# Splitting the first quarter of w1 into a free buffer ahead of the experts, loading the second tile's rows later, and re-dealing the routing turns

## The chip, the cores and the metric

One core of one Trainium2 chip runs the whole program. The metric is the device time of one execution in microseconds (us). A core has five engines with queues of their own: TensorE (PE, with its weight loads PEld), VectorE (DVE), ScalarE (ACT), GpSimd (POOL) and SyncE (SP), which here issues the plain DMAs. POOL issues the indirect ones. Each queue runs in order.

## The reference

Attention with a bias, then a mixture of experts with one expert for each token. q, k, v are (8, 8, 576, 64); the 4608 tokens have 512 columns; there are 8 experts with w1 (512 x 1024) and w2 (1024 x 512).

```python
scores = scale * q @ k.T + bias            # bias from positions: log1p, a 32-wide hidden layer, 8 heads
attn = softmax(scores); x = attn @ v       # rows of 512 columns, one for each token
logits = x @ w_gate + modality_bias[modality_id]
e_idx = argmax(logits); gate = softmax(logits)[e_idx]
for e in range(8):                         # only the rows with e_idx == e
    out[mask] = gate[mask] * (relu(x[mask] @ w1[e]) @ w2[e])
```

## The kernel before, in words

**Attention.** The kernel works on 32 pairs of heads, four pairs for each of the 8 batches. The loop of `attention` takes a pair in five turns (u = 0 to 4) and runs one turn past the last pair: pair 32 only finishes the products with v of pair 31. What PE, ACT, DVE, POOL and SP do in a turn is written out by hand in `ORDER`; letters X and B in it give a turn to the routing of the batch before. Extra work of the last pairs is hung on turns by `first_tiles`, which fills a table (pair, u) -> functions.

**Routing.** For each batch `route_steps` gives two lists: PE steps (X: two logits steps, two transposes of the logits, the rank, five `s_rows`) and other steps (B: reciprocal, top, one-hot, gate, position, and for the last batch the tables of the experts' tiles). A step waits for a given number of steps of the other list. `s_rows(c)` transposes 128 rows of x (64 for c = 4), scales them on POOL and scatters them by an indirect DMA (L904) into `xg`, a table in HBM sorted by expert. All accesses to `xg` at rows known only at run time are ordered one after the other: a scatter waits until the transfer before it has landed, a load of rows (L1125) waits for the scatters before it, and a later scatter waits for that load.

**Experts.** Tiles of 256 rows: K = 5 first tiles, which hold only rows of the first seven batches, run in `moe_first`, with the routing of the eighth batch dealt out among them. Then `moe_rest` runs the others. `load_rows(t)` (SP, L1125) brings 256 rows of `xg`; `xprep` transposes them on PE (L1202) and splits them into a high and a low part, `xh` on ACT (L1205) and `xl` on DVE (L1206). These lie in the two buffers QT[0] and QT[1], which attention used for q; tile t takes number t % 2. The weights are split the same way into `whi` and `wlo`. `phase1` makes the hidden layer in four pieces (f2 = 0 to 3) of 24 matmuls (L1221), each followed by a relu on ACT (L1223) and its low part on DVE (L1224). `phase2` (L1238) makes two halves of 128 rows with 24 matmuls each; between them stands `xprep` of the next tile. After phase 1 the next tile's w1 is split (four casts on ACT and four subtractions on DVE, L1185 and L1186).

**The first tile's w1** has no phase before it in which to be split. So `wsplit_cols(part)` splits one quarter of its columns at a time (256 of 1024, which is what one f2 needs): the cast on ACT at L1192, the subtraction on DVE at L1193. `tile(0)` calls it for parts 0 and 1 ahead of f2 = 0, for part 2 ahead of f2 = 1 and for part 3 ahead of f2 = 2. The target `whi`, `wlo` lies in the pool "mp", which takes the memory of attention's own pool (Eb, eT, the rows `xrb` that are scattered from, and others). The first use of the new pool waits for every user of the old one, the last scatter's DMA among them.

**The routing turns of the first tiles** are the list `steps` in `moe_first`: six entries for a tile, one behind each f2, one behind the first half of phase 2 and `xprep`, one behind the second half. B and X give a turn to the lists above, F writes one of nine fills (`fill_steps`): one blank block, and behind each expert's last row one tile of blank rows (L1151 on SP).

**Sums over experts.** `s_cum` in `table` and `s_keep` form running sums over 8 values with one copy and seven one-element additions on DVE (L1014, L1016, L1081, L1083).

Of the kernel before, what the change touches and what calls it, by code (L numbers as in the profile page):

```python
# [11 lines left out]
F32 = mybir.dt.float32  # L12
# [9 lines left out]
P = 128  # L22
# [7 lines left out]
E = 8  # L30
# [80 lines left out]
class Attn:  # L111
# [819 lines left out]
    def moe_early(self, cp):  # L931

        nc = self.nc
        lo, hi = n_tiles(self.n_tok)
        self.n_kt = self.n_tab // TS - 1
        self.T = hi
        self.sure = lo
        n_tt = max(E, hi + 1 - self.K)
        one = cp.tile([1, 2 * E + self.n_kt + n_tt], F32, name="one")
        nc.sync.dma_start(one, self.io["c_one"])  # L940
        self.eb, self.iota = one[:, 0:E], one[:, E : 2 * E]
        self.kt, self.tt = one[:, 2 * E : 2 * E + self.n_kt], one[:, 2 * E + self.n_kt :]
        self.gates = cp.tile([P, 4], F32, name="gates")
        self.gk = cp.tile([1, E, self.n_kt], F32, name="gk")
        self.ge = cp.tile([1, n_tt, E], F32, name="ge")
        self.tf = cp.tile([1, 4, n_tt], F32, name="tabf")
        self.ev = {nm: cp.tile([1, E], F32, name=nm) for nm in ("cnt", "off", "nt", "cum", "val", "taken", "start", "big")}
        self.ex = cp.tile([1, 1], F32, name="last_expert")
        nc.vector.memset(self.ex, -1.0)
        nc.vector.memset(self.ev["taken"], 0.0)  # L950
        self.tabs = {nm: cp.tile([1, 4, n], I32, name=f"tab_{nm}") for nm, n in (("first", max(1, self.K)), ("big", hi + 1 - self.K), ("tiny", E))}
        self.idt = cp.tile([P, 4], I32, name="idt")
        self.tab_end = cp.tile([1, E], I32, name="tab_end")
        self.ids_q = [cp.tile([P, 1], I32, name=f"idsq{k}") for k in range(NT)]
        self.quad = cp.tile([P, 1], F32, name="quad")
        nc.sync.dma_start(self.quad, self.io["c_quad"])

        slots = self.NBm.rearrange("p (c q h) k -> p c q (h k)", c=4, q=NP)
        w = [slots[:, :, q, 0 : 2 * DM] for q in range(NP)]
        rest = [slots[:, :, q, 2 * DM : 2 * S] for q in range(NP)]  # L960
        self.wst, self.ws = [w[0], w[1]], [w[2], w[3]]
        self.xr = [slots[:, c, 2, XW * j : XW * j + XW] for c, j in ((0, 0), (1, 0), (3, 0), (0, 1), (1, 1))]
        self.lt = slots[:, 2, 2, 0:XW]
        self.hq = [rest[0], rest[3]]
        self.gx = [self.NBr[:, k : k + 2, 0:XW] for k in (0, 2)]
        d = self.n_pair % 2
        qt = [self.QT[k].rearrange("p a w -> p (a w)") for k in (d, 1 - d)]
        self.xh = [t[:, 0 : NDC * TS].rearrange("p (c w) -> p c w", c=NDC) for t in qt]
        self.xl = [t[:, NDC * TS : 2 * NDC * TS].rearrange("p (c w) -> p c w", c=NDC) for t in qt]
# [19 lines left out]
    def counts(self, out, least):  # L989
# [9 lines left out]
        )  # L999
        V.tensor_reduce(out, self.gk, axis=AX.X, op=ALU.add)  # L1000

    def table(self, nm, nt, start):


        V, ev = self.nc.vector, self.ev
        tab = self.tabs[nm]
        T = tab.shape[2]
        TE = [1, T, E]
        f, ge, tt = self.tf[:, :, 0:T], self.ge[:, 0:T, :], self.tt[:, 0:T]
        row = lambda t: t.rearrange("p (o e) -> p o e", o=1).to_broadcast(TE)  # L1010
        col = lambda t: t.rearrange("p (t o) -> p t o", o=1).to_broadcast(TE)

        def s_cum():
            V.tensor_copy(ev["cum"], nt)  # L1014
            for e in range(1, E):
                V.tensor_tensor(ev["cum"][:, e : e + 1], ev["cum"][:, e : e + 1], ev["cum"][:, e - 1 : e], op=ALU.add)  # L1016
            V.tensor_tensor(ev["val"], nt, ev["cum"], op=ALU.subtract)
            V.scalar_tensor_tensor(ev["val"], ev["val"], float(TS), start, op0=ALU.mult, op1=ALU.add)
            V.tensor_tensor(ev["val"], ev["val"], self.eb, op=ALU.add)

        def s_expert():
            V.tensor_tensor(ge, col(tt), row(ev["cum"]), op=ALU.is_ge)
            V.tensor_reduce(f[:, 0, :], ge, axis=AX.X, op=ALU.add)
            V.tensor_scalar(f[:, 3, :], f[:, 0, :], E - 0.5, None, op0=ALU.is_lt)
            V.tensor_scalar(f[:, 0, :], f[:, 0, :], E - 1.0, None, op0=ALU.min)

        def s_row():
            V.tensor_tensor(ge, col(f[:, 0, :]), row(self.iota), op=ALU.is_equal)
            V.tensor_tensor(ge, ge, row(ev["val"]), op=ALU.mult)
            V.tensor_reduce(f[:, 1, :], ge, axis=AX.X, op=ALU.add)  # L1030
            V.scalar_tensor_tensor(f[:, 1, :], tt, float(TS), f[:, 1, :], op0=ALU.mult, op1=ALU.add)
            if nm != "tiny":
                V.tensor_tensor(f[:, 1, :], f[:, 1, :], f[:, 3, :], op=ALU.mult)
                return

            empty = float(E * self.n_tab)
            V.scalar_tensor_tensor(f[:, 1, :], f[:, 1, :], -empty, f[:, 3, :], op0=ALU.add, op1=ALU.mult)
            V.tensor_scalar(f[:, 1, :], f[:, 1, :], empty, None, op0=ALU.add)
            V.tensor_copy(tab[:, 0:2, :], f[:, 0:2, :])
            V.tensor_copy(tab[:, 3, :], f[:, 3, :])  # L1040

        def s_new():
            V.tensor_tensor(f[:, 2, 0:1], f[:, 0, 0:1], self.ex, op=ALU.is_equal)
            if T > 1:
                V.tensor_tensor(f[:, 2, 1:T], f[:, 0, 1:T], f[:, 0, 0 : T - 1], op=ALU.is_equal)
            V.tensor_scalar(f[:, 2, :], f[:, 2, :], -1.0, 1.0, op0=ALU.mult, op1=ALU.add)
            V.tensor_tensor(f[:, 2, :], f[:, 2, :], f[:, 3, :], op=ALU.mult)
            V.tensor_copy(self.ex, f[:, 0, T - 1 : T])
            V.tensor_copy(tab, f)

        return [s_cum, s_expert, s_row] + ([s_new] if nm != "tiny" else [])
# [17 lines left out]
    def last_tables(self):  # L1069
# [8 lines left out]
            V.tensor_tensor(ev["nt"], ev["cnt"], ev["start"], op=ALU.is_gt)  # L1078

        def s_keep():  # L1080
            V.tensor_copy(ev["cum"], ev["nt"])  # L1081
            for e in range(1, E):
                V.tensor_tensor(ev["cum"][:, e : e + 1], ev["cum"][:, e : e + 1], ev["cum"][:, e - 1 : e], op=ALU.add)  # L1083
            V.tensor_tensor(ev["big"], ev["big"], ev["nt"], op=ALU.add)
            V.scalar_tensor_tensor(ev["nt"], ev["cum"], NT + 0.5, ev["nt"], op0=ALU.is_lt, op1=ALU.mult)
            V.tensor_tensor(ev["big"], ev["big"], ev["nt"], op=ALU.subtract)
# [101 lines left out]
    def wsplit_cols(self, part):  # L1188

        sl = slice(TS * part, TS * part + TS)  # L1190
        w, h, l = self.wst[0][:, :, sl], self.whi[0][:, :, sl], self.wlo[0][:, :, sl]
        self.nc.scalar.copy(h, w)  # L1192
        self.nc.vector.tensor_tensor(l, w, h.bitcast(F32), op=ALU.subtract)  # L1193

# [13 lines left out]
    def phase1(self, t, before, beside):  # L1208
        nc = self.nc
        xh, xl = self.xh[t % 2], self.xl[t % 2]  # L1210
        hh, hl = self.hh, self.hl
        hi, lo = self.whi[0], self.wlo[0]
        for f2 in range(NFC // 2):
            before(f2)
            ps = self.ring("p1")
            for a in range(2):
                f = 2 * f2 + a
                fs = slice(P * f, P * f + P)
                ops = [(w, x, c) for w, x in ((hi, xh), (hi, xl), (lo, xh)) for c in range(NDC)]
                for i, (w, x, c) in enumerate(ops):  # L1220
                    nc.tensor.matmul(ps[:, a, :], w[:, c, fs], x[:, c, :], start=i == 0, stop=i == len(ops) - 1)  # L1221
            sl = slice(2 * f2, 2 * f2 + 2)
            nc.scalar.activation(hh[:, sl, :], ps, AF.Relu)  # L1223
            nc.vector.scalar_tensor_tensor(  # L1224
                hl[:, sl, :], ps, 0.0, hh[:, sl, :].bitcast(F32), op0=ALU.max, op1=ALU.subtract
            )
            beside()
# [28 lines left out]
    def tile(self, t, beside=None, between=()):  # L1256
# [10 lines left out]
        def ahead(f2):  # L1267
            for f in itertools.islice(between, 1):
                f()
            if t:  # L1270
                return
            for part in {0: (0, 1), 1: (2,), 2: (3,)}.get(f2, ()):
                self.wsplit_cols(part)
            if f2 == 2:
                self.load_new(1, 0)
# [20 lines left out]
    def first_tiles(self):  # L1296
# [12 lines left out]
        add(3, 0, lambda: self.load_w("first", 0, 1, self.wst[1]))  # L1309
        for w in range(2):  # L1310
            add(4, w, lambda w=w: self.xprep(0, w))
        if self.K > 1:
            add(4, 0, lambda: self.load_rows(1))
        return at

    def route_rest(self):
# [5 lines left out]
    def moe_first(self):  # L1322


        steps = iter("B,X,X,X,X,B,B,X,B,B,X,X,X,X,X,B,BF,BFF,BF,BF,BF,BF,BBF,BF".split(","))

        def beside():
            for op in next(steps, ""):
# [2 lines left out]
                    f()  # L1331

        self.fills = iter(self.fill_steps())
        if self.K:
            self.moe_load(1)
        for t in range(self.K):
# [166 lines left out]
```

## Time and profile before

| | |
|---|---|
| time, median of 3 runs | 1111.91 us (1110.93 to 1113.19) |
| the profiled execution's own time | 1110.05 us |
| its span, first to last instruction | 1108.1 us |
| mean granted TensorE clock | 0.990 of full speed |
| DVE, ACT, POOL busy | 764.6, 647.9 and 316.5 us |

All rows below are of this one execution; their times are us from the start of its span. Attention ends and the experts begin around 640 us. The first five tiles start phase 1 at 645.5, 674.4, 704.4, 729.1 and 752.5 us. In a timeline a row has its start, its length, the engine, the line, the operation, output <- input, the shape, the count, and in brackets the engine's idle time before it with what ended it. A letter q behind an engine's name is its queue.

### The profile page before, as it was taken

What the parts mean: (1) busy time and instruction counts of PE and PEld (TensorE: products, weight loads), DVE (VectorE), ACT (ScalarE), POOL (GpSimd) and SP (SyncE); (2) the same over time, 40 slices, a digit from 0 to 9 for tenths busy, and PEclk for the clock granted to TensorE, in tenths of its full rate; (3) what the DMA queues carried; (4) which work ended last, traced back from release to release, by engine and by line L of the source; (5) the groups of instructions that cost most, each with busy time, mean ns of one, the idle gap of its engine ahead of it and who ended that gap; (6) DMA issues with size and microseconds to landing.
All of it is one profiled execution on the core that took longest, in us unless ns stands there. A gap on an engine that the chain in (4) does not pass through costs nothing.

```text
span 1108.1 us, 23130 instructions
## 1 busy us (share of the span) xinstructions
PE 1062.6 (96%) x8324; PEld 890.5 (80%) x8324; DVE 764.6 (69%) x1682; ACT 647.9 (58%) x1250; POOL 316.5 (29%) x546
## 2 busy tenths in 40 slices
PE   7989999999999999999999978999999999999994
PEld 3457888878788887878777868899999999889894
DVE  7976678787687877867778655697555654454553
ACT  7766766666675766666666643454555544454542
POOL 0003425525345344363452411421101011111010
PEclk9999999999999999999999989999999999999998
DMA  6994444536445353544444601134113721243310
GB/s 167 223 191 98 122 112 109 149 82 166 95 122 135 100 149 96 131 126 123 119 125 109 215 24 39 68 132 156 55 39 114 273 71 57 75 164 108 122 40 22
DMA packets 88765, 128.09 MB, mean 116 GB/s; under 512 B 30753, under 2 KB 55585, under 8 KB 88643
## 3 DMA queue, kind: packets, MB, share of 16 engines
q1 hardware_dynamic: 82626, 107.58, 36.2%
q0 software_dynamic: 5920, 18.95, 4.8%
q8 instruction: 68, 1.11, 0.4%
q14 instruction: 55, 0.44, 0.1%
q10 hardware_dynamic: 96, 0.00, 0.0%
HBM read 135.62 MB, written 23.44 MB: 144 GB/s over the span
## 4 chain that ended last, share of the span: by engine, by line
PE 81%; DVE 5%; DMA 5%; POOL 5%; issue 2%; ACT 2%; SPq 0%; POOLq 0%; ACTq 0%; DVEq 0%
PE p L1221 18%; PE p L1238 17%; PE xps L545 12%; PE sps L453 10%; PE eps L497 7%; PE xps L402 4%; PE xps L539 3%; PE bps L199 3%; POOL qs L384 2%; DMA xg<-xrb,pos 1%; DMA NBm<-xTb 1%; PE eps L503 1%; PE xps L1202 1%; POOL xg L904 1%; DVE Eb L468 1%
## 5 line engine op out<-in xcount | busy, mean ns | idle before, releaser
L482 ACT ACTIVATE Eb<-Eb,mn 128x576 f32<-128x576 f32 x288 | 222.8, 776 | 146.8 <-DVE mn L468 144.8
L453 PE MATMUL sps<-KT,QT 128*128 128x288 f32 x1152 | 204.2, 312 | 4.5 <-DVE mn L468 2.8
L468 DVE CUSTOM_DVE_ANT_0 Eb<-sps,NBm 128x576 f32<-128x576 f32 x256 | 185.6, 753 | 10.7 <-issue 4.3
L1221 PE MATMUL p<-QT,w1hi 128*128 128x256 f32 x1152 | 165.4, 287 | 6.0 <-ACT w1hi L1192 6.0
L453 PEld LDWEIGHTS sps<-KT,QT 128*128 128x128 f32 x1152 | 161.7, 189 | 10.1 <-issue 3.4
L1221 PEld LDWEIGHTS p<-QT,w1hi 128*128 128x128 f32 x1152 | 151.0, 194 | 10.9 <-ACT w1hi L1192 6.5
L1224 DVE SCALAR_TENSOR_TENSOR hl<-p,hh 128x512 fp32r<-128x512 f32 x72 | 49.7, 691 | 152.9 <-ACT hh L1223 152.7
L497 PE MATMUL eps<-idf,Eb 128*128 128x128 f32 x1024 | 143.8, 275 | 0.0
L545 PE MATMUL xps<-eT,vraw 128*64 128x288 f32 x1024 | 141.8, 412 | 0.5 <-DVE KT L340 0.5
L1247 POOL DMA_INDIRECT out<-mo,idt x36 | 41.6, 1156 | 320.3 <-ACT QT L1205 225.1
L487 POOL COPY rem<-Eb 128x128 f32<-128x128 f32 x128 | 36.9, 295 | 315.9 <-ACT Eb L482 315.5
L497 PEld LDWEIGHTS eps<-idf,Eb 128*128 128x128 f32 x1024 | 113.5, 140 | 6.2 <-DVE mn L468 5.0
L338 ACT ACTIVATE eT<-eps 128x512 f32<-128x512 f32 x160 | 94.2, 590 | 41.0 <-PE eps L497 41.0
L1223 ACT ACTIVATE hh<-p 128x512 fp32r<-128x512 f32 x72 | 43.0, 598 | 125.1 <-PE p L1221 122.4
L1238 PE MATMUL p<-w2hi,hh 128*128 128x512 f32 x288 | 114.0, 396 | 0.0
L1238 PE MATMUL p<-w2hi,hl 128*128 128x512 f32 x288 | 112.5, 390 | 0.0
L545 PEld LDWEIGHTS xps<-eT,vraw 128*64 128x64 f32 x1024 | 65.2, 136 | 48.4 <-issue 12.3
L340 DVE COPY xTb<-xps 128x288 f32<-128x288 f32 x64 | 29.2, 457 | 107.5 <-PE xps L545 61.6
L1186 DVE TENSOR_TENSOR w2lo<-NBm,w2hi 128x1024 fp32r<-128x1024 f32 x72 | 88.2, 1225 | 16.4 <-ACT w2hi L1185 16.4
L1221 PE MATMUL p<-QT,w1lo 128*128 128x256 f32 x576 | 93.6, 285 | 0.0
L340 DVE COPY eT<-eps 128x512 f32<-128x512 f32 x128 | 84.6, 682 | 0.0
L1186 DVE TENSOR_TENSOR w1lo<-NBm,w1hi 128x1024 fp32r<-128x1024 f32 x72 | 83.2, 1218 | 0.0
(227 smaller groups left out, 1842.1 us busy)
## 6 DMA issues: line engine op xcount, KB each, us to landing
NBm<-moe_w SPq DMA_DIRECT2D x23, 2048.0 KB
NBm<-moe_w SPq DMA_DIRECT2D x44, 1024.0 KB
QT<-QT SPq DMA_DIRECT2D x64, 304.0 KB
NBr<-xg SPq DMA_DIRECT2D x20, 516.0 KB
NBm<-xTb SPq DMA_DIRECT2D x32, 288.0 KB
KH<-KT SPq DMA_DIRECT2D x64, 144.0 KB
qraw<-q SPq DMA_DIRECT2D x32, 256.0 KB
kraw<-k SPq DMA_DIRECT2D x32, 256.0 KB
```

Source lines behind the costliest of these rows:

```text
L338: self.nc.scalar.activation(out, ps, AF.Copy, scale=scale)
L340: self.nc.vector.tensor_copy(out, ps)
L402: nc.tensor.transpose(pr[:, j, :], xs[:, 4 * (part % 2) + j, :, :].rearrange("p a d -> p (a d)"), self.idr)
L453: nc.tensor.matmul(ps[:, half, :], q, k[:, HS * half : HS * half + HS], start=i == 0, stop=i == len(terms) - 1, skip_group_check=True,)
L468: nc.vector.tensor_tensor_reduce(out=e.rearrange("p (t w) -> p t w", t=2), in0=ps, in1=nb.rearrange("p (t w) -> p t w", t=2), scale=1.0, s ...
L482: self.nc.scalar.activation(e, e, AF.Exp, bias=mn, scale=-1.0, accum_out=sm)
L497: nc.tensor.transpose(ps[:, k, :], e[:, part, P * k : P * k + P], self.idf)
L545: nc.tensor.matmul(ps[o, :], v[:, h, k, :], self.eT[:, h, k, sl], start=half == 1 and k == 0, stop=half == 0 and k == 3, tile_position=(0, ...
L1186: self.nc.vector.tensor_tensor(l, w, h.bitcast(F32), op=ALU.subtract)
L1221: nc.tensor.matmul(ps[:, a, :], w[:, c, fs], x[:, c, :], start=i == 0, stop=i == len(ops) - 1)
L1224: nc.vector.scalar_tensor_tensor(hl[:, sl, :], ps, 0.0, hh[:, sl, :].bitcast(F32), op0=ALU.max, op1=ALU.subtract)
L1238: nc.tensor.matmul(ps, h[:, f, sl], m[:, f, :], start=i == 0, stop=i == len(ops) - 1)
```

## The change

Four edits, which stand in the diff below.

1. **First quarter of w1.** Part 0 is split no longer into `whi[0]`, `wlo[0]` but into `xh[1]`, `xl[1]`, that is the buffer QT[1], and this is called at turn (32, 3), in front of the last products with v. `phase1` reads this buffer for f2 = 0 of tile 0. Part 1 alone is split ahead of f2 = 0.
2. **Rows of the second tile.** `load_rows(1)` moves from turn (32, 0) to the start of `moe_first`, behind all scatters of the seventh batch.
3. **Routing turns.** The list `steps` of `moe_first` is dealt out anew. By tile, before: (B,X,X,X,X,B) (B,X,B,B,X,X) (X,X,X,B,BF,BFF) (BF,BF,BF,BF,BBF,BF); after: (B,X,X,X,-,X) (BB,-,X,B,B,X) (X,X,X,X,BBF,BBFF) (BF,BF,BF,BF,BBF,BF).
4. **Running sums.** Three additions of 8 values, shifted by 1, 2 and 4 within zero-padded rows, replace the copy and seven additions. Three small memsets are added in `moe_early`.

```diff
+        self.pad = [cp.tile([1, 4 + E], F32, name=f"pad{k}") for k in range(3)]
+        for t in self.pad:
+            nc.vector.memset(t, 0.0)
+        self.ev["nt"] = self.pad[0][:, 4:]
...
+    def running(self):
+        n, a, b = self.pad
+        for out, x, k in ((a[:, 4:], n, 1), (b[:, 4:], a, 2), (self.ev["cum"], b, 4)):
+            self.nc.vector.tensor_tensor(out, x[:, 4:], x[:, 4 - k : 4 - k + E], op=ALU.add)
...
-            V.tensor_copy(ev["cum"], nt)
-            for e in range(1, E):
-                V.tensor_tensor(ev["cum"][:, e : e + 1], ev["cum"][:, e : e + 1], ev["cum"][:, e - 1 : e], op=ALU.add)
+            self.running()
...
-        w, h, l = self.wst[0][:, :, sl], self.whi[0][:, :, sl], self.wlo[0][:, :, sl]
+        w = self.wst[0][:, :, sl]
+        h, l = (self.whi[0][:, :, sl], self.wlo[0][:, :, sl]) if part else (self.xh[1], self.xl[1])
...
+            early = t == 0 and f2 == 0
+            hi, lo = (self.xh[1], self.xl[1]) if early else (self.whi[0], self.wlo[0])
...
-            for part in {0: (0, 1), 1: (2,), 2: (3,)}.get(f2, ()):
+            for part in {0: (1,) if self.K else (0, 1), 1: (2,), 2: (3,)}.get(f2, ()):
...
-        if self.K > 1:
-            add(4, 0, lambda: self.load_rows(1))
+        add(4, 3, lambda: self.wsplit_cols(0))
...
-        steps = iter("B,X,X,X,X,B,B,X,B,B,X,X,X,X,X,B,BF,BFF,BF,BF,BF,BF,BBF,BF".split(","))
+        steps = iter("B,X,X,X,,X,BB,,X,B,B,X,X,X,X,X,BBF,BBFF,BF,BF,BF,BF,BBF,BF".split(","))
...
         self.fills = iter(self.fill_steps())
+        if self.K > 1:
+            self.load_rows(1)
```

## Rows read from the trace of the kernel before

**Rows 1.** The page's busy times: us, share of the span, instructions
```profile
PE 1062.6 (96%) x8324; PEld 890.5 (80%) x8324; DVE 764.6 (69%) x1682; ACT 647.9 (58%) x1250; POOL 316.5 (29%) x546
```

**Rows 2.** Stretches: length, busy PE, PEld, DVE, ACT, POOL, clock, DMA share, GB/s
```profile
639.50:645.50 6.00, 0.02 (x1) 0.00 (x0) 0.46 (x1) 1.07 (x2) 1.26 (x3) 0.71 0.16 45
645.50:647.50 2.00, 1.98 (x9) 1.98 (x10) 2.00 (x2) 0.92 (x1) 0.00 (x0) 0.50 0.00 0
647.50:649.50 2.00, 2.00 (x14) 2.00 (x14) 0.36 (x1) 0.00 (x0) 0.00 (x0) 0.66 0.00 0
...
680.30:682.10 1.80, 0.19 (x2) 0.10 (x1) 1.53 (x10) 1.53 (x2) 0.22 (x1) 1.00 0.00 0
682.10:684.10 2.00, 1.97 (x13) 1.97 (x13) 1.97 (x5) 0.00 (x0) 0.00 (x0) 0.72 0.03 8
684.10:686.10 2.00, 2.00 (x11) 2.00 (x11) 0.12 (x2) 0.00 (x0) 0.00 (x0) 0.50 0.00 0
```

**Rows 3.** Timeline of the passage from attention to the experts
```profile
635.70 0.18 POOL L903 COPY xrb<-gi 64x4 f32<-64x4 f32 x1
...
636.03 0.22 ACT L338 ACTIVATE rT<-eps 128x64 f32<-128x64 f32 x1 [0.66 <-PE eps L508]
...
636.94 0.46 DVE L340 COPY xTb<-xps 128x288 f32<-128x288 f32 x1 [1.83 <-PE xps L545]
...
638.77 0.75 PE L539 MATMUL xps<-rT,vrem 128*128 128x288 f32 x2
...
641.37 0.95 POOL L904 DMA_INDIRECT xg<-xrb,pos  x1 [5.49 <-DMA NBr<-xg]
...
644.43 1.99 ACT L1192 CAST w1hi<-NBm 128x1024 fp32r<-128x1024 f32 x2 [8.17 <-DMA xg<-xrb,pos]
...
645.52 2.08 PE L1221 MATMUL p<-QT,w1hi 128*128 128x256 f32 x8 [6.01 <-ACT w1hi L1192]
```

**Rows 4.** The chain that ended last, in order of time: start, us, what
```profile
622.30 6.33 DMA xg<-xrb,pos
...
636.64 3.94 DMA NBr<-xg
...
652.98 1.00 PE xps L800 x8
...
752.61 11.51 PE p L1221 x96
```

**Rows 5.** Timeline, DVE in the first tile: first hl, and w1's last quarter
```profile
650.77 0.69 DVE L1224 SCALAR_TENSOR_TENSOR hl<-p,hh 128x512 fp32r<-128x512 f32 x1 [2.91 <-ACT hh L1223]
...
656.97 1.22 DVE L1193 TENSOR_TENSOR w1lo<-NBm,w1hi 128x1024 fp32r<-128x1024 f32 x1
```

**Rows 6.** Timeline of PE: transposes of routing that waited in tiles 0 and 1
```profile
668.77 0.33 PE L823 MATMUL xps<-idf,lt 128*128 128x128 f32 x1 [1.55 <-DVE QT L1206]
...
698.05 0.66 PE L893 MATMUL xps<-idf,xTb 128*128 128x128 f32 x4 [2.06 <-DVE QT L1206]
```

**Rows 7.** Timeline: running sums on DVE, and PE behind the first of them
```profile
576.93 2.36 DVE L1016 TENSOR_TENSOR cum<-cum 1x1 f32<-1x1 f32 x7
...
580.64 1.48 PE L453 MATMUL sps<-KT,QT 128*128 128x288 f32 x8 [1.66 <-DVE mn L468]
...
729.61 1.24 DVE L1083 TENSOR_TENSOR cum<-cum 1x1 f32<-1x1 f32 x7
```

**Rows 8.** Timeline of tiles 2 to 4: scatters, fills, the sixth tile's rows
```profile
707.82 1.01 POOL L904 DMA_INDIRECT xg<-NBm,pos  x1 [0.28 <-POOL NBm L903]
...
724.39 1.78 POOL L904 DMA_INDIRECT xg<-NBm,pos  x1 [1.43 <-DMA xg<-NBm,pos]
...
729.58 0.38 SPq L1141 DMA_DIRECT2D xg<-NBm  x1
...
763.26 0.63 SPq L1125 DMA_DIRECT2D NBr<-xg  x1
...
769.43 0.82 PE L1202 MATMUL xps<-idf,NBr 128*128 128x128 f32 x6
```

More of the change, by code (lines that the diff above doesn't have):

```diff
@@ L946, in moe_early @@
         self.tf = cp.tile([1, 4, n_tt], F32, name="tabf")
-        self.ev = {nm: cp.tile([1, E], F32, name=nm) for nm in ("cnt", "off", "nt", "cum", "val", "taken", "start", "big")}
+        self.ev = {nm: cp.tile([1, E], F32, name=nm) for nm in ("cnt", "off", "cum", "val", "taken", "start", "big")}
+        self.pad = [cp.tile([1, 4 + E], F32, name=f"pad{k}") for k in range(3)]
+        for t in self.pad:
+            nc.vector.memset(t, 0.0)
+        self.ev["nt"] = self.pad[0][:, 4:]
         self.ex = cp.tile([1, 1], F32, name="last_expert")
@@ L1080, in s_keep @@
         def s_keep():
-            V.tensor_copy(ev["cum"], ev["nt"])
-            for e in range(1, E):
-                V.tensor_tensor(ev["cum"][:, e : e + 1], ev["cum"][:, e : e + 1], ev["cum"][:, e - 1 : e], op=ALU.add)
+            self.running()
             V.tensor_tensor(ev["big"], ev["big"], ev["nt"], op=ALU.add)
@@ L1211, in phase1 @@
         hh, hl = self.hh, self.hl
-        hi, lo = self.whi[0], self.wlo[0]
         for f2 in range(NFC // 2):
             before(f2)
+            early = t == 0 and f2 == 0
+            hi, lo = (self.xh[1], self.xl[1]) if early else (self.whi[0], self.wlo[0])
             ps = self.ring("p1")
@@ L1217, in phase1 @@
                 f = 2 * f2 + a
-                fs = slice(P * f, P * f + P)
+                fs = slice(P * (f % 2 if early else f), P * (f % 2 if early else f) + P)
                 ops = [(w, x, c) for w, x in ((hi, xh), (hi, xl), (lo, xh)) for c in range(NDC)]
```

## The prediction

> **What bounds the kernel now.** I read the busy times first: TensorE is busy 1062.6 of 1108.1 us [rows 1], so only what makes PE idle or slow can move the time, and the reader should look for the rest of 45 us. [...] The timeline and the chain tell why the passage is idle [rows 3, 4]. The second tile's rows are loaded as soon as the last scatter but one has landed, from 636.64 for 3.94 us, to 640.58; POOL, ready with the last scatter's rows at 635.88, waits 5.49 us for that load and scatters at 641.37; ACT casts at 644.43 what PE needs at 645.52. Meanwhile PE's last product with v ends at 638.77 + 0.75 = 639.52. Two more waits are transposes of routing behind DVE: 1.55 and 2.06 us [rows 6]. In the attention part one wait of 1.66 us follows the running sums [rows 7]. From 704 us on the tiles run without a gap: 96 products of phase 1 in 11.51 us, 2.88 for a piece of 24 [rows 4].
>
> **The change part by part.** The sum goes against the profiled execution, 1110.05 us (span 1108.1 and 1.95 around it); the median shown is 1.86 above that, and I add the sum to the median.
>
> *Passage, edits 1 and 2.* The cast of part 0 writes a buffer outside the old pool. ACT is free from 636.25 [rows 3]; a cast takes 1.0 (half of 1.99), so it is done at 637.3. DVE copies until 637.40, then subtracts for 1.22 [rows 3, 5], to 638.6. Both are hidden by the last products, which end at 639.52; without this cover they would cost 2.2. The next DVE copy of attention waits for PE until after 639.5 anyway. So the first products can follow at once: of the 6.0 idle us 0.1 stay, **-5.9**. PE doesn't pause, so the slow clock behind the gap goes as well: 2.0 x (1 - 0.50) + 2.0 x (1 - 0.66) = 1.7 [rows 2], **-1.7**.
>
> What is late next is part 1, still behind the old pool. Without the load in between, the last scatter starts 0.8 us after the landing that let the load go at 636.6 (as at 641.37 behind 640.58), at 637.4; from its start to the cast took 3.06 us [rows 3], so the cast begins at 640.5 and ends at 641.5, the subtraction at 642.7. PE has finished the first piece at 639.5 + 2.9 = 642.4 and needs the low part 1.0 us later: in time by 0.9 and 0.7. Behind that DVE is the tight engine: from its first hl to the end of the last quarter it worked 658.19 - 650.77 = 7.4 us [rows 5]. Now hl starts 0.6 us behind the first piece, at 643.0, and the last quarter is ready at 650.4; PE, after two pieces (5.8) and both logits steps (1.0 for the first [rows 4]; the second has an eighth of its columns, I take 0.3), needs it at 642.4 + 7.1 + 1.0 = 650.5. Even, so I put **+0.3**; bounds 0 and 2.7 (the last scatter taking 6.33, as one did [rows 4], instead of about 3).
>
> The load itself goes behind the scatter, 640.2 to 644.1; on SP nothing is queued behind it before tile 0's own transfers, and its reader `xprep(1)` comes after all of phase 1. Nothing.
>
> *Routing turns, edit 3.* In tile 0 the transpose that stood behind `xprep` and waited for the subtractions of w1 and xl now stands behind the second half of phase 2, when DVE is long done: **-1.55** [rows 6]. In tile 1 the rank came one piece behind the one-hot and PE waited: 1.80 - 0.19 = 1.6 idle, and 2.0 x 0.28 + 2.0 x 0.50 = 1.56 lost to the clock [rows 2]. Now top and one-hot both stand behind the first piece and the rank two pieces, 5.8 us, after it. DVE must do hl (0.7), one subtraction (1.2) and twelve small operations, which at the ten in 1.53 of [rows 2] and gaps between them are some 2.6 us; with the relu before them that is 5.2. In time by about 0.5; I leave 0.3 for a wait: **-2.9**, bounds -3.2 and -1.6 (a wait as long, without the fall of the clock). In tile 1 the first rows of the last batch leave the place behind `xprep`, where they waited 2.06 for xl: **-2.1** [rows 6].
>
> This has a price. The scatters of the last batch begin one turn later. Of the five, the second now takes the place that the third had, and the last has one more in front of it in tile 2. From the scatter at 707.82 to the last at 724.39 there are three steps in 16.57 us, one load of rows (3.94) among them [rows 4, 8]: 4.2 for a scatter. Behind the last one hangs a chain without slack: POOL's blank block, stored at 729.58, eight fills and two loads of rows on SP, the second at 763.26, landed about 767.2; PE transposes these rows at 769.43 [rows 8]. The slack is 2.2, and tile 2 grows by four transposes (0.66 at most [rows 6], I take 0.4). So PE will wait 4.2 - 2.2 - 0.4 = **+1.6** in tile 4; bounds 0 and 5.
>
> *Running sums, edit 4.* Seven additions take 1.24 us when undisturbed, 0.177 each [rows 7]; a copy and seven become three, five fewer, 0.9 us. Two of the three places are hidden in tiles that PE bounds. The first, at 576.93, is followed by a PE wait of 1.66 on DVE: **-0.9**, bounds 0 and -1.66 (there the seven took 2.36). [...] The three memsets, where PE waits for DVE once, cost **+0.1** (0 to 0.3, by the same 0.177 at most for two of them).
>
> Sum: -5.9 - 1.7 + 0.3 - 1.55 - 2.9 - 2.1 + 1.6 - 0.9 + 0.1 = **-13.05**. The profiled execution goes from 1110.05 to 1097.0, the median from 1111.91 to **1098.9**.
>
> **The rivals.**
> (a) *The chain of scatters and fills is longer than 4.2 more.* Each later link adds to the wait in tile 4, and from about 1 us more also to that for tile 4's own rows. With 3 us more: 1101.9; with 5: 1103.9. For it: there is no slack in the chain; against: single steps of it were even.
> (b) *Part 1 comes late.* The last scatter takes 6.33 us, the cast starts at 643.8 and the second piece 2.4 to 2.7 us late: 1101.5. Against it: the last one itself took 3.06 with all waits behind it [rows 3].
> (c) *The early quarter does not do what it says*, because PE's first product waits for the scatter all the same (its PSUM bank too was attention's). Then the products start at 640.5 rather than 639.6, or, if the early cast itself is held, at 641.5: 1099.8 to 1100.8.
> (d) *Slower.* The scatters of the last batch and the fills behind them get slow as a whole: five scatters at 6.33 in place of about 3.06 are 16 us more, all of it waited for before the sixth tile's transposes: 1115. It decides from 13 us of added delay, 0.8 us for each of the 16 links; between 11 and 15 there is no change to be measured. For it: one scatter did take 6.33 [rows 4]; against: the steps in tile 2 averaged 4.2 with issue and landing [rows 8], and nothing in the change adds traffic beside them. [...]
>
> **How the numbers follow.** The forecast has 0.62, its own range is 1096.5 to 1101. Rival (a) has 0.15, (b) 0.10, (c) 0.06, (d) 0.07. All bounds at their best give -16.3 (1095.6), all but (d) at their worst about -4 (1108). The range 1095.5 to 1104.5 takes in the forecast, most of (a), (b) and (c), and leaves out (d) and the far ends. What a measurement can tell from no change is 0.2%, 2.2 us. Only (d) reaches that: 0.03 for no change, 0.04 for slower, 0.93 for faster.
>
> **What would show it.** Right: the first L1221 starts within 0.3 us of the last L539, at about 639.5, clock 1.00 there; the last scatter near 637.4 with no wait for a load; L823 and the rank without idle time before them; a new wait of PE at the L1202 of tile 4, for the load of rows. Wrong: a PE gap over 1 us between the first two pieces (b); a first product at 640.5 or later (c); any clock below 1.00 between 640 and 700; a wait of more than 4 us in tiles 3 to 4 (a, d). If tile 2's start does not move by 14 us or so, the sum fails before the chain is reached.

## The result, and the profile after

The changed kernel takes 1101.74 us (median of 4 runs, 1101.56 to 1102.27), the kernel before 1112.11 beside it (4 runs, 1110.93 to 1113.19): ratio 0.9908, 95% interval 0.9891 to 0.9925. It is faster by some 10 us; the forecast of 1098.9 was 2.8 us too low, the range held it. The profiled execution took 1102.27 us (span 1100.5), 7.8 less than the one profiled before, where the sum of the prediction, which is worked against that execution, has 13.05 less.

In the busy times little is to be seen: the busy line of the page, to be read against [rows 1], has PE 1.7 us and DVE 2.7 us less.

```profile
PE 1060.9 (96%) x8324; PEld 889.9 (81%) x8324; DVE 761.9 (69%) x1665; ACT 647.6 (59%) x1250; POOL 318.9 (29%) x546
```

The timeline of the passage answers to [rows 3].

```profile
635.20 1.04 ACT L1199 CAST QT<-NBm 128x1024 fp32r<-128x1024 f32 x1
635.57 0.95 POOL L904 DMA_INDIRECT xg<-xrb,pos  x1 [1.37 <-DMA xg<-xrb,pos]
...
637.78 0.75 PE L539 MATMUL xps<-rT,vrem 128*128 128x288 f32 x2
638.15 3.25 PE L1229 MATMUL p<-QT,QT 128*128 128x256 f32 x24
...
638.61 1.05 ACT L1199 CAST w1hi<-NBm 128x1024 fp32r<-128x1024 f32 x1 [2.37 <-PE xps L539]
```

The early cast is done at 636.24, POOL no longer waits for the second tile's rows (5.49 us before), and the first piece of the experts follows the last product with v at once. No gap is left there.

The chain that ended last shows what took its place. It is PE from 638 to 716, and then no longer PE: it goes over POOL (an output scatter of 1.97 us, with the blank rows behind it) and SP into the row table's transfers, and comes back to PE at 760.22. Columns: start, us, what.

```profile
638.53 5.75 PE p L1229 x48
...
672.70 0.04 PE xps L871
...
717.68 1.97 POOL out L1255
...
720.80 0.38 SPq L1147
...
728.61 3.92 DMA NBr<-xg
...
752.29 3.75 DMA xg<-NBm
...
756.17 4.00 DMA NBr<-xg
760.17 0.04 issue
760.22 1.97 PE xps L1209 x8
```

The rank (L871) is a link of 0.04 us in PE's own chain, with no wait. Two PE waits are new, both at the transposes of a tile's rows: in tile 3 for those of tile 4, in tile 4 for those of tile 5 (timeline of PE):

```profile
732.58 1.97 PE L1209 MATMUL xps<-idf,NBr 128*128 128x128 f32 x8 [2.60 <-DMA NBr<-xg]
...
760.22 1.97 PE L1209 MATMUL xps<-idf,NBr 128*128 128x128 f32 x8 [2.62 <-DMA NBr<-xg]
```

The stretches around them, with the columns of [rows 2]:

```profile
642.00:644.00 2.00, 2.00 (x20) 2.00 (x18) 1.69 (x2) 1.92 (x3) 0.00 (x0) 1.00 0.00 0
...
730.60:732.60 2.00, 0.02 (x1) 0.02 (x1) 1.08 (x1) 2.00 (x3) 0.00 (x0) 0.91 0.61 223
732.60:734.20 1.60, 1.60 (x9) 1.60 (x9) 1.60 (x3) 1.60 (x2) 0.00 (x0) 0.50 0.33 110
734.20:736.20 2.00, 2.00 (x8) 1.63 (x7) 2.00 (x3) 1.67 (x4) 0.52 (x1) 0.64 0.46 171
760.20:762.00 1.80, 1.78 (x9) 1.79 (x10) 1.80 (x2) 1.80 (x3) 0.00 (x0) 0.50 0.71 235
762.00:764.00 2.00, 2.00 (x8) 1.64 (x8) 2.00 (x3) 1.32 (x3) 0.88 (x1) 0.76 0.01 5
```

In the passage the granted clock is now 1.00; behind each new wait it is 0.50, then 0.64 behind the first and 0.76 behind the second. Each wait is paid 1.6 times: tiles 3 and 4 take 27.61 and 27.47 us from the first piece of one to that of the next, 4.3 and 4.2 more than before, for waits of 2.6.

By the starts of phase 1 (before: in the section on its profile, and 775.76 for tile 5; after: 638.15, 663.82, 687.71, 712.84, 740.45, 767.92) tile 2 begins 16.7 us earlier, tile 5 only 7.8. From there on both have the same pace, 23.3 us a tile.

Why the chain was late shows in POOL's and DVE's timeline of tile 2:

```profile
699.70 1.46 POOL L904 DMA_INDIRECT xg<-NBm,pos  x1 [4.13 <-DMA NBr<-xg]
...
703.85 5.76 POOL L904 DMA_INDIRECT xg<-NBm,pos  x1 [1.49 <-DMA xg<-NBm,pos]
704.10 4.61 DVE L1192 TENSOR_TENSOR w1lo<-NBm,w1hi 128x1024 fp32r<-128x1024 f32 x4
...
712.70 1.02 POOL L904 DMA_INDIRECT xg<-NBm,pos  x1 [1.88 <-DMA xg<-NBm,pos]
...
716.43 0.94 POOL L904 DMA_INDIRECT xg<-NBm,pos  x1 [1.51 <-DMA xg<-NBm,pos]
```

The third of the five scatters takes 5.76 us instead of about 1.0, and ends 0.90 us after a run of four subtractions on DVE with both inputs in SBUF (704.10 + 4.61 = 708.71). From its start to that of the fourth is 8.85 us, where I had 4.2 for a step. That the run holds the scatter is what the experiments had to show.

### The profile page after: what moved, and what is told of

Its sections match the earlier page's. It is cut to its first block, busy times and chain, and to the rows that moved or that the text cites. A ratio compares the mean times of both kernels' runs of the same rounds, so it can differ in the third digit from the quotient of the medians.

```text
span 1100.5 us, 23117 instructions
## 1 busy us (share of the span) xinstructions
PE 1060.9 (96%) x8324; PEld 889.9 (81%) x8324; DVE 761.9 (69%) x1665; ACT 647.6 (59%) x1250; POOL 318.9 (29%) x546
## 4 chain that ended last, share of the span: by engine, by line
PE 81%; DMA 7%; POOL 5%; DVE 4%; issue 1%; ACT 1%; SPq 0%; POOLq 0%; ACTq 0%; DVEq 0%
PE p L1246 16%; PE p L1229 16%; PE xps L545 12%; PE sps L453 11%; PE eps L497 7%; PE xps L402 4%; PE xps L539 3%; PE bps L199 3%; DMA xg<-NBm 3%; POOL qs L384 2%; PE xps L1209 1%; PE eps L503 1%; POOL xg L904 1%; DMA NBm<-xTb 1%; DVE Eb L468 1%
## 5 line engine op out<-in xcount | busy, mean ns | idle before, releaser
L1229 PE MATMUL p<-QT,w1hi 128*128 128x256 f32 x1136 | 161.0, 284 | 0.0
L1229 PEld LDWEIGHTS p<-QT,w1hi 128*128 128x128 f32 x1136 | 146.9, 191 | 3.8 <-issue 1.8
L1229 PE MATMUL p<-QT,w1lo 128*128 128x256 f32 x568 | 91.3, 283 | 0.0
```

## The experiments

Theory: the change gains 16 to 17 us up to tile 2 and gives 8 to 9 back in tiles 3 and 4. The later turns make the chain of scatters and fills late, and DVE's run makes it later by another 4 to 5 us. Rivals: the 5.76 us are the DMA's own; any busy DVE does it; the waits have a cause outside the turns. The kernel before ran at 1113.5 to 1114.2 us on the chips of these runs, so ratios to it are compared. Each trace is of one execution.

| kernel | us | ratio, 95% interval |
|---|---|---|
| changed | 1101.74 | 0.9908 (0.9891 to 0.9925) |
| changed, again | 1102.88 | 0.9897 (0.9868 to 0.9926) |
| old turns | 1102.56 | 0.9893 (0.9871 to 0.9915) |
| edit 1 alone | 1111.07 | 0.9972 (0.9957 to 0.9986) |
| edit 2 alone | 1108.03 | 0.9947 (0.9929 to 0.9964) |
| edit 4 alone | 1111.74 | 0.9983 (0.9964 to 1.0001) |
| no subtractions | 1098.61 | 0.9861 (0.9840 to 0.9881) |
| copies from PSUM | 1099.38 | 0.9866 (0.9846 to 0.9885) |
| two subtractions | 1101.38 | 0.9876 (0.9849 to 0.9903) |
| fills dealt out anew | 1094.36 | 0.9824 (0.9807 to 0.9841) |
| the same without edit 1 | 1097.78 | 0.9845 (0.9816 to 0.9874) |
| fills anew, table moved | 1094.30 | 0.9815 (0.9789 to 0.9842) |

**Old turns (edits 1, 2 and 4).**

```diff
-"B,X,X,X,,X,BB,,X,B,B,X,X,X,X,X,BBF,BBFF,BF,BF,BF,BF,BBF,BF"
+"B,X,X,X,X,B,B,X,B,B,X,X,X,X,X,B,BF,BFF,BF,BF,BF,BF,BBF,BF"
```

> The changed kernel with the old list of routing turns (edits 1, 2 and 4 stay). Theory (the turns gained as much in tiles 0 and 1 as the later chain gave back in tiles 3 and 4): the first product stays at 638.2 us and tile 0 keeps no gap; PE waits again for about 1.55, 1.6 and 2.06 us in tiles 0 and 1 and its clock falls once there, so tile 2 starts about 6 us later than in the changed kernel, at 694; but no PE wait for a load of rows in tiles 3 and 4, 8 us less there. In all 1100 to 1102, within 2 us of the changed kernel's 1101.7. Rival 1 (the turns are a clear gain, as predicted, -5 us): 1106.5 to 1108. Rival 2 (the passage moved every scatter forward, and the waits in tiles 3 and 4 have another cause): waits over 2 us there in this kernel too, 1108.

PE's waits in its timeline:

```profile
660.43 0.33 PE L823 MATMUL xps<-idf,lt 128*128 128x128 f32 x1 [1.57 <-DVE QT L1213]
...
673.10 0.18 PE L871 MATMUL xps<-ohb,tri 128*128 128x48 bf16 x1 [1.10 <-POOL ohb L856]
...
688.23 0.66 PE L893 MATMUL xps<-idf,xTb 128*128 128x128 f32 x4 [2.05 <-DVE QT L1213]
...
760.12 1.09 PE L1209 MATMUL xps<-idf,NBr 128*128 128x128 f32 x8 [0.38 <-DMA NBr<-xg]
```

The waits of [rows 6] and the rank's are back, tile 2 starts at 694.57 instead of 687.71, but tile 5 at 766.53, earlier than in the changed kernel: one wait of 0.38 us is all there is in tiles 3 and 4. Edit 3 gained 6.5 us (from the first piece to tile 2: 56.04 against 49.56) and gave 8.25 back (tiles 2 to 4: 71.96 against 80.21). The ratios of the whole, 0.9893 and 0.9908, can't be told apart: on balance no worth of edit 3 is shown. The clock stayed at 1.00 behind the rank's wait here, where it had fallen before, so my theory's "its clock falls once" missed. With edit 1 or edit 2 alone it fell in tile 1 too, but behind the other wait there (0.71 and 0.50, 0.78 and 0.50).

**Edits 1 and 2, each alone** in the kernel before: for edit 1 the lines of `wsplit_cols`, `phase1`, `tile` and the call at (4, 3) in the diff above; for edit 2 the two places of `load_rows(1)`.

> The kernel before with edit 1 alone (early first quarter; the second tile's rows stay in front of the last scatter). Theory: PE's first piece runs from about 639.5 to 642.7 without a gap, then PE waits for part 1, whose cast begins at 644.4 as in the kernel before, until about 645.4: a gap of 2.7 to 3 us in place of 6, and the slow clock behind it stays. Gain about 3.2 us, 1108.5 to 1109.5. Rival (the first piece waits for the last scatter all the same, and the gain came from edit 2 alone): first product behind 641 us, 1111 to 1112.

> The kernel before with edit 2 alone (second tile's rows loaded behind the last scatter; the first quarter still goes into the pool w1hi). Theory: the last scatter starts near 636 us, the first cast near 639, the first product at 639.7 to 640.5 instead of 645.5; PE idles 0.5 to 1.5 us there. Gain 5 to 6.5 us, 1105 to 1107: nearly all that the passage gained needs edit 2 alone, edit 1 adds only some 1.5 us. Rival (the two are needed together, as the sum of the prediction had them): the gain stays below 3 us, 1109 or more.

Edit 1 alone, then edit 2 alone:

```profile
641.90 3.25 PE L1223 MATMUL p<-QT,QT 128*128 128x256 f32 x24
...
647.36 1.04 ACT L1193 CAST w1hi<-NBm 128x1024 fp32r<-128x1024 f32 x1 [7.37 <-DMA xg<-xrb,pos]
...
648.45 2.08 PE L1223 MATMUL p<-QT,w1hi 128*128 128x256 f32 x8 [3.30 <-ACT w1hi L1193]
```

```profile
640.25 0.95 POOL L904 DMA_INDIRECT xg<-xrb,pos  x1 [1.60 <-DMA xg<-xrb,pos]
...
643.28 2.00 ACT L1192 CAST w1hi<-NBm 128x1024 fp32r<-128x1024 f32 x2 [4.20 <-DMA xg<-xrb,pos]
...
644.38 1.21 PE L1221 MATMUL p<-QT,w1hi 128*128 128x256 f32 x8 [2.03 <-ACT w1hi L1192]
```

With edit 1 alone the gap stands one piece later, 3.30 us in place of 6.01. With edit 2 alone 2.03 us of it are left, more than the 0.5 to 1.5 expected. (The last product with v starts 2.8 us later in both than before. These edits act only from about 630 us on, and 0.9 to 1.0 us of it stands already ahead of the running sums' wait near 580, the rest arises there and in the slow clock behind it.) From that product's start to tile 1 it takes 35.63 us before, 34.04 with edit 1, 30.51 with edit 2, 27.93 with both (and edit 4): gains of 1.6, 5.1 and 7.7. Edit 2 is most of the passage; the rival that needs both together has 1.0 us.

**Edit 4 alone** (`running` and the memsets of the diff).

> The kernel before with edit 4 alone (three shifted additions and three memsets). The prediction's step: -0.9 + 0.1, so 1111.3 against 1112.1 for the kernel before. What the changed kernel's trace suggests (the wait behind the first running sums fell from 1.66 to 1.17 us): -0.5, and attention ends 0.5 to 1 us earlier. Rival (the wait is set by something else on VectorE): no change, within 0.3 us.

The ratio's interval reaches from -4.0 us to 0.1: it holds the -0.8 of the prediction and can't tell it from nothing. In this trace the last product with v starts 0.2 us earlier than before, not the 0.5 to 1 expected. The trace of the changed kernel shows where the wait of 1.66 us [rows 7] comes from, and why it is not gone:

```profile
577.31 1.41 POOL L384 TENSOR_TENSOR ks<-kraw,ks 128x576 fp32r<-128x576 f32 x1
577.46 1.27 DVE L1026 SCALAR_TENSOR_TENSOR val<-val,start 1x8 f32<-1x8 f32 x1
...
579.71 1.48 PE L453 MATMUL sps<-KT,QT 128*128 128x288 f32 x8 [1.17 <-DVE mn L468]
```

An operation on 8 values just behind the sums, elsewhere 0.15 us, takes 1.27 and ends with POOL's subtraction (577.31 + 1.41 = 578.72, 577.46 + 1.27 = 578.73). It looks like the same hold with the engines exchanged; the last kernel below tries it. With the eight old operations PE waited 2.10 and 2.14 us there in the kernels with edit 1 and edit 2 alone, and the clock then fell to 0.70 and 0.62; behind the 1.66 of before, with the same eight, and the 1.17 here it stayed at 1.00.

**No subtractions, copies from PSUM, two subtractions.** All three are the changed kernel with another DVE run in tile 2; what is left out would write the values that stand there already (tiles 2 and 3 have one expert).

```diff
+    def wsplit(self, k, part, w=None, low=True):
...
+        if low:
+            self.nc.vector.tensor_tensor(l, w, h.bitcast(F32), op=ALU.subtract)
...
-            self.wsplit(0, c)
+            self.wsplit(0, c, low=t != 2)              # none; two: low=t != 2 or c < 2
+        if t == 2:                                     # copies only
+            for _ in range(7):
+                self.nc.vector.tensor_copy(self.hq[0], self.p1[self.at["p1"] % 3].rearrange("p a (c w) -> p (a c) w", c=2))
```

> The changed kernel without the four subtractions (two inputs in SBUF) that make w1lo for the fourth tile, the run in tile 2 from 704.10 to 708.71; they would write the values that already stand there. Theory (the third scatter of the last batch was held by this run until it ended): that scatter takes 1.0 to 1.5 us instead of 5.76, the chain behind it comes 4 to 4.6 us earlier, the two PE waits of 2.60 and 2.62 us in tiles 3 and 4 go, and with them the slow clock behind each: 1095 to 1097. Rival A (the 5.76 us are the DMA's or the memory's own): the scatter stays over 4 us, 1101.5. Rival B (the chain is limited elsewhere, by the output scatter and the memset of the blank rows on GpSimd): scatter short but the waits only 1 us shorter, 1099 to 1101.

> As the kernel without the four subtractions, but in their place seven copies of 512 columns from PSUM on VectorE, about 0.68 us each, 4.8 us in all (a harmless copy into an unused buffer). Theory (what holds the scatter is a VectorE operation with two SBUF inputs, not a busy VectorE): scatter 1.0 to 1.5 us, time as without the subtractions, 1095 to 1097. Rival (any back-to-back VectorE work of that length holds it): scatter over 4 us, 1101.5.

> The changed kernel without the last two of the four w1lo subtractions in tile 2 (they would write the values that already stand there), so that the run is about 2.3 us long. Theory (the scatter is released about 0.9 us behind the end of the run): scatter 3.3 to 3.6 us in place of 5.76; everything behind it 2.3 us earlier; the wait in tile 3 falls from 2.60 to about 0.3 and its slow clock with it, the one in tile 4 stays at 2.2 to 2.6; 1098 to 1099.5. Rival (the hold has one length, whatever the run): 5.8 or 1.0.

Without subtractions; with copies; with two:

```profile
704.97 1.02 POOL L904 DMA_INDIRECT xg<-NBm,pos  x1 [0.74 <-POOL NBm L903]
...
756.16 1.31 PE L1210 MATMUL xps<-idf,NBr 128*128 128x128 f32 x8 [2.22 <-DMA NBr<-xg]
```

```profile
704.57 5.03 DVE L1294 COPY NBm<-p 128x512 f32<-128x512 f32 x7
704.66 1.02 POOL L904 DMA_INDIRECT xg<-NBm,pos  x1 [1.84 <-DMA xg<-NBm,pos]
```

```profile
704.60 3.52 POOL L904 DMA_INDIRECT xg<-NBm,pos  x1 [1.46 <-DMA xg<-NBm,pos]
...
704.87 2.34 DVE L1193 TENSOR_TENSOR w1lo<-NBm,w1hi 128x1024 fp32r<-128x1024 f32 x2
...
758.88 1.97 PE L1210 MATMUL xps<-idf,NBr 128*128 128x128 f32 x8 [4.17 <-DMA NBr<-xg]
```

The hold is settled: no run, 1.02 us; a run half as long, 3.52 (expected 3.3 to 3.6); a DVE busy for 5.03 us from PSUM, 1.02. In the half run the scatter ends at 708.12, again 0.91 us after the last subtraction. The two rivals on the scatter fall; the third, on the waits, fell with the old turns. Whether a DVE operation with a single input, in SBUF, would hold it too no run here tries.

The price was not as I had expected: 1095 to 1097 us was forecast for the first two. The wait in tile 3 goes in all three, but one in tile 4 stays, of 2.22 us without subtractions and 1.92 with copies, and with two subtractions it is 4.17, more than the 2.62 of the changed kernel. The two waits do not add up. Both hang on one chain, and PE can't go on into tile 5 before the chain's last link, the load at 756.17 in the changed kernel, has landed. What PE did not wait for in tile 3 it waits for in tile 4. Only the end of the chain counts. From the start of tile 2 it comes after 72.51 us in the changed kernel, 4.67 earlier without the run and 2.11 earlier with half of it, near what the scatter is shorter by (4.74 and 2.24), and tile 5 starts 4.34 and 2.08 earlier. The medians go the same way (ratios 0.9861 and 0.9876; 1098 to 1099.5 was expected for the latter, 1101.38 measured beside 1102.88 for the changed kernel), though the latter's interval does not part it from the changed kernel. Behind the one wait that is left without the run the clock is slow (columns of [rows 2]):

```profile
756.16:758.00 1.84, 1.84 (x10) 1.74 (x11) 1.84 (x2) 1.84 (x3) 0.00 (x0) 0.70 0.71 256
758.00:760.00 2.00, 2.00 (x6) 1.52 (x6) 2.00 (x3) 1.23 (x3) 0.96 (x1) 0.50 0.00 0
```

**The changed kernel again**, beside the kernel with two subtractions.

> The changed kernel once more, beside the next three on one chip, since the earlier comparisons were made on two chips. Theory and rivals alike: 1101 to 1103, third scatter of the last batch over 4 us, waits of about 2.6 us for the loads of rows in tiles 3 and 4. If this scatter takes 1 us here, the hold is a matter of chance in the start, not of the order of work.

```profile
702.85 5.82 POOL L904 DMA_INDIRECT xg<-NBm,pos  x1 [1.43 <-DMA xg<-NBm,pos]
```

The waits are 3.14 and 2.52: in this order of work the hold is not chance.

**Fills dealt out anew.**

```diff
-"B,X,X,X,,X,BB,,X,B,B,X,X,X,X,X,BBF,BBFF,BF,BF,BF,BF,BBF,BF"
+"B,X,X,X,,X,BB,,X,BBBF,FF,FX,X,X,X,X,B,BB,BF,BF,BF,BF,BBF,BF"
```

> The changed kernel with other turns: the last batch's gate, position and count go behind the last piece of tile 1, the blank block and three fills in front of the last batch's first scatter, the five others into tile 3: (B,X,X,X,-,X) (BB,-,X,BBBF,FF,FX) (X,X,X,X,B,BB) (BF,BF,BF,BF,BBF,BF). Theory (tiles 3 and 4 wait only because the chain of fills and loads of rows hangs behind the last scatter): no PE wait for a load of rows in tiles 3 and 4, tiles 2 and 3 some 25 and 23.5 us, 1093 to 1095. Rival (the fills in tile 1 delay the first scatters as much): waits of 1 to 3 us in tiles 2 to 4, 1098 to 1101.

```profile
705.69 5.58 POOL L904 DMA_INDIRECT xg<-NBm,pos  x1 [1.66 <-DMA xg<-NBm,pos]
705.76 4.61 DVE L1192 TENSOR_TENSOR w1lo<-NBm,w1hi 128x1024 fp32r<-128x1024 f32 x4
```

The scatter is held as in the changed kernel, but with four fills (and three B turns) moved in front of the scatters it costs nothing: tiles 2 to 4 take 25.13, 23.35 and 23.31 us, without a PE wait. 1094.36 us, some 7 to 9 less than the changed kernel (by the medians and by the ratios), 19 less than the kernel before beside it. So the 8 us or so given back in tiles 2 to 4 were the chain's.

**The same without edit 1.** Undone as in the diff of the change.

> The version with the fills dealt out anew (1094.4), with edit 1 undone: parts 0 and 1 of w1 both ahead of the first piece, into the pool. Theory from the kernel with edit 2 alone (PE wait 2.03 us at the first product): a wait of 2 us there, possibly some slow clock behind it, 1096.5 to 1097.5. Rival (edit 1 brings nothing once the rows are loaded later, because VectorE is the tight engine in tile 0 anyway): within 0.5 of 1094.4.

```profile
639.40 1.22 PE L1227 MATMUL p<-QT,w1hi 128*128 128x256 f32 x8 [1.18 <-ACT w1hi L1198]
```

PE waits 1.18 us at the first product, where 2 was expected, and tile 0 takes 0.2 more; the medians differ by 3.4 us, the ratios by 0.002 with intervals that overlap. From the last product with v to tile 1, edit 1 is worth 1.75 us by these traces, 2.6 by those of edit 2 alone and of both above.

**Fills anew, table moved.**

```diff
-            add(*divmod(4 + k, 5), f)
+            add(*divmod((4, 6, 7, 8, 9, 11)[k], 5), f)
```

> The version with the fills dealt out anew (1094.4), and the steps of the first table hung on turns (0,4), (1,1), (1,2), (1,3), (1,4), (2,1) in place of (0,4) to (1,4), so that the running sums no longer meet GpSimd's subtraction of two SBUF inputs in turn (1,0). Theory (that subtraction holds one small VectorE operation for about 1.1 us, and PE then waits 0.85 to 1.7 us behind DVE at the scores): no small VectorE operation of that table takes over 0.4 us but the mask of 144 values in (0,4), the PE wait of about 1.1 us near 581 goes, attention ends 0.8 to 1.2 us earlier: 1093.3. Rival (the work only moves, and another turn gets the wait): 1094 to 1095.

DVE and POOL where the running sums stood, and where they stand now:

```profile
577.29 1.42 POOL L384 TENSOR_TENSOR ks<-kraw,ks 128x576 fp32r<-128x576 f32 x1
...
577.97 0.99 DVE L777 TENSOR_SCALAR rs<-sums 128x9 f32<-128x9 f32 x4
...
580.30 0.16 DVE L1010 TENSOR_TENSOR cum<-pad 1x8 f32<-1x8 f32 x1
```

POOL's subtraction now holds another operation, one with a single tensor as input (0.99 against 0.38), which nobody waits for; the PE wait near 580 is gone. The time, 1094.30, where 1093.3 was expected, can't be told from 1094.36: the wait's removal is shown in the trace, its worth not.

## Why the prediction was right, and where it was not

**Passage, -7.3** (gap -5.9, clock -1.7, part 1 +0.3): measured -7.7 with the old turns, of it 6.4 up to the first product and 1.3 in tile 0. Right, and part 1 was in time: PE's first two pieces stand without a gap. Rivals (b) and (c) did not come.

**Turns in tiles 0 and 1, -6.55:** measured -6.5 against the old turns. The waits went as forecast, but that the sum fits is in part luck: the clock behind the rank, which I had at 1.56 of it, did not fall in the profile of the old turns, so that the comparison does not hold this term. In its place stand the four transposes that left tile 1 (0.44), which I had counted as added to tile 2 and not as taken from tile 1, 0.3 more in tile 0 than forecast, and the wait of 0.3 at the rank that did not come; some 0.4 stays open.

**Running sums, -0.9 + 0.1:** attention's last product with v starts 1.0 us earlier in the changed kernel's profile, but 0.2 with this edit alone, and anywhere from 636.8 to 639.4 us in the kernels that have it (638.8 before): the size is not shown. The reason was only half right: I counted instructions at 0.177, and missed that one small operation there waits out a POOL subtraction in either kernel (before, one of the seven additions took 1.27 us where the others took 0.15; after, the operation on 8 values 1.27).

**The chain of scatters and fills, +1.6, bounds 0 and 5:** this term failed, in size: tiles 2 to 4 gave back 8.25 us against the old turns, 8.8 against the kernel before. Three things were wrong in it.

First, "4.2 for a scatter". It was an average over three steps of before, carried to a new place in tile 2 without looking at what DVE does there. The step is 8.85 when DVE's run falls on it. The rows were there, in the trace of before: the last scatter of [rows 8] took 1.78 us, not 1.0, inside such a run, and the third took 2.06 beside one subtraction. The three steps were 4.0 (without the load), 4.95 and 3.66 us, not even, as rival (a) has it.

```profile
715.78 2.06 POOL L904 DMA_INDIRECT xg<-NBm,pos  x1 [3.54 <-DMA NBr<-xg]
...
722.98 4.63 DVE L1186 TENSOR_TENSOR w1lo<-NBm,w1hi 128x1024 fp32r<-128x1024 f32 x4
```

The changed kernel's trace has the hold in both directions: the scatter took 5.76 us with DVE's run beside it, and an operation on 8 values 1.27 us beside POOL's subtraction. I had weighed neither.

Second, the wait's price. I counted a wait of 1.6 us as 1.6. Without the hold it was 2.22 us, near the forecast, and tile 4 grew by 4.09 (27.40 against 23.31), since the clock stood at 0.5 to 0.7 behind it. I had priced just this at the passage and not at the wait that I added.

Third, tile 3. That its rows would be late too "from about 1 us more" stood in rival (a) as an addition. The runs show that it isn't one: the end of the chain sets the time, however the waits are split.

What came about is the mechanism of rival (a): one step of the chain longer by 4.65 us (8.85 in place of 4.2), which by that rival's sum adds 1.6 + 4.65 = 6.25 us, and measured 8.8, for the second reason. That the time still fell into the range is in part luck. The gain up to tile 2 was 16.7 us, 2 more than my 14.65. And the execution profiled before was 2.1 us faster than the median beside it, the one after 0.5 slower, so that the medians differ by 10.4 us and the profiles by 7.8. Against 7.8 the sum of 13.05 misses by 5.3. One small slip in the ranges: with every bound at its best the terms give -16.1, not -16.3.

## What to carry to other kernels

When steps are moved along a chain that has no slack, price each link at its new place: what runs on the other engines at that moment, and not the mean of the old places. A wait that is added can cost more than its length, here 4.1 us for 2.2, by the slow clock behind it, and two waits on one chain cost what its last link costs: with two subtractions the first wait went and the second grew from 2.62 to 4.17. If a chain is late, look for links that do not need to stand where they are: four fills moved ahead of the scatters, with three B turns, took 8.4 us out of tiles 2 to 4, more than the redealing of turns had gained in tiles 0 and 1.

## What the hardware showed that I had not expected

Indirect DMAs on POOL that started beside a DVE subtraction with two SBUF inputs were held. From 640 us on in the profiles of before and after, 41 of them, scatters to the table and to the output alike, start while such a subtraction runs, and all end 0.82 to 0.97 us after the end of that subtraction, even where the next one follows at once (a run's inner ends are worked out from its length, 1.14 us apart); 27 more, in the timelines of eight other kernels, end 0.86 to 0.96 us after it. So the scatter of 1.78 us in the kernel before got in between the second and the third subtraction of its run, and the output scatter in the changed kernel's chain took 1.97 beside one at 717.54.

Those that waited out a whole run (5.76, 5.82, 5.58, 5.55 and 5.83 us, and 3.52 for a run of two) all started 0.04 to 0.31 us ahead of its first subtraction. In two other kernels one that started 0.14 us ahead of a single subtraction, or 0.04 behind its start, took 1.03. What makes the difference is open. If it is the start, a few tenths of a us decide over some 4 us of the chain; no run moves a scatter by so little.

The DVE copies from PSUM held nothing (the scatter took 1.02 us beside 5.03 us of them), and a DVE operation with one input in PSUM and one in SBUF did not either: the scatter at 716.43 took 0.94 beside it (timeline of the changed kernel).

```profile
716.60 0.69 DVE L1232 SCALAR_TENSOR_TENSOR hl<-p,hh 128x512 fp32r<-128x512 f32 x1 [0.26 <-ACT hh L1231]
```

In the other direction a POOL subtraction held a DVE operation of 8 values until it ended, 1.27 us for 0.15.

The rows here show no release, only the end of the POOL instruction some 0.9 us after the subtraction, and an undisturbed one lasts 0.94 to 1.04 us.
